# A deeper opening: normalise, transpose and values in three successive turns

## The chip, the cores and the metric

The kernel runs on one core of one Trainium2 chip. The metric is device time in microseconds of one execution. The core's engines work side by side, each in its own order: TensorE (PE, with PEld for its weight loads) multiplies, VectorE (DVE), ScalarE (ACT) and GpSimd (POOL) work on elements, SyncE (SP) issues loads and stores. They wait for each other only through semaphores.

## The reference

A windowed attention over 8 sequences of 576 positions and 8 heads of 64, followed by a feed-forward block with the function h * tanh(softplus(h)) between two weight matrices.

```python
scores = scale * np.matmul(q, k.transpose(0, 1, 3, 2))
mask = (rel >= 0) & (rel < window)          # window = 64
scores = np.where(mask, scores, -1000000000.0)
attn = np.exp(scores - np.max(scores, axis=-1, keepdims=True))
attn = attn / (np.sum(attn, axis=-1, keepdims=True) + 1e-09)
attn_out = np.matmul(attn, v)
...
h = x @ w_in                                # 4608 x 512, 512 x 2048
g = h * np.tanh(np.where(h > 20.0, h, np.log1p(np.exp(np.minimum(h, 20.0)))))
out = g @ w_out                             # 2048 x 512
```

## The kernel before

The 4608 tokens are cut into chunks of 384. For each chunk the attention is computed for four pairs of heads and gives x; then 16 steps, one for each 128 columns of w_in, compute h = x w_in into `h_ps`, apply the function, and add the product with w_out into `acc`. Numbers are kept as two parts, a rounded high one and the remainder (`xh`, `xl`; `gh`, `gl`; two halves of `wi`; `wo_h`, `wo_l`), so each product takes three matmuls.

The weights come as 64-bit numbers and are made into such pairs on the chip, one piece of 128 x 512 after another, by `stream()`. A piece takes: a scaling on ACT (`w_scale`), a shift and a clamp on DVE (`w_ready`, TENSOR_SCALAR), two joins on DVE (`w_joined`, SCALAR_TENSOR_TENSOR), a rounding to the high part (`w_round`, a CAST), and the difference that is the remainder (`w_rest`, TENSOR_TENSOR wi<-st,wi or wo_l<-st,wo_h), which also issues the load of a later piece into the freed buffer. `some(n)` runs the next n operations of this stream; `OPS[u]` is how many in turn u. The pieces are w_in 0, w_in 1, w_out 0, w_in 2, w_out 1 and so on.

The opening, which is all that the change touches, works through the first two chunks: eight units u = 0 to 7 (chunk, head pair), U = 8. A unit needs

- `products_of(u)`: 24 score matmuls, s_ps (12 instructions); they issue the load of a later unit's q and k once their buffers are free
- `masks(u)`: on DVE six operations that add the mask, scale and find the minimum, pr<-s_ps,masks; `exps(u)`: six exponentials on ACT, which also sum
- `summed(u)`: add of 1e-9 on POOL, reciprocal on DVE, and POOL's multiply pr<-pr,sm of 768 columns
- `transposed(u)` on TensorE (t_ps), `copied(u)` to pT, the first half by ACT, the second by DVE
- `values_of(u)`: 24 matmuls into o_ps; `rest_high(u)` (ACT, xh) and `rest_low(u)` (DVE, xl) cut the result in two parts.

A loop over turns writes these out. Everything here goes through wrappers that keep each engine in the order of the code, so a waiting instruction holds up all that stands behind it on its engine. Between the units, `first_parts` places the matmuls of steps 0 to 2 (`PARTS`: step and number of matmuls) and `step` their functions; step 0 and 1 read x of chunk 0, step 2 x of chunk 1. After the opening the steps follow each other, a step of h_ps, a step of acc.

The functions that the diff touches or that call them:

Of the kernel before, what the change touches and what calls it, by code (L numbers as in the profile page):

```python
# [11 lines left out]
F32 = mybir.dt.float32  # L12
# [4 lines left out]
ALU = mybir.AluOpType  # L17
# [3 lines left out]
OFFSET = 2.0 ** -112  # L21
# [9 lines left out]
def tile_window_attn_mish_ffn(  # L31
# [57 lines left out]
    vec, act, pool, load = (InTurn(e) for e in (nc.vector, nc.scalar, nc.gpsimd, nc.sync))  # L89
# [48 lines left out]
    def in_order():  # L138
        return tc.issue_after(order[-1]) if order else nullcontext()
# [4 lines left out]
    def acc_bank(t, name):  # L144
        return ps_acc.tile([P, CH], F32, name=name, tag=f"acc{t}")

    def h_bank(name, width=CH):
        return ps_h.tile([P, width], F32, name=name, tag="h_ps")
# [5 lines left out]
    def at_bank(name, width=CH):  # L154
        at_last[0] = next(at_turn)
        return ps_at.tile([P, width], F32, name=name, tag=f"at{at_last[0]}")

    def at_set(n, name):
        return ps_at.tile([P, DO], F32, name=name, tag=f"at{n}")
# [120 lines left out]
    BY_HEAD = [(h, m) for h in range(2) for m in range(NM)]  # L280
# [107 lines left out]
    def residue():  # L388
        while residues:
            gl, t, gh = residues.pop(0)  # L390
            vec.tensor_tensor(gl, t, gh.bitcast(F32), ALU.subtract)
# [48 lines left out]
    def w_load():  # L440
        if pieces:
            fn, f = pieces.pop(0)
            loaded.append(fn(f))
# [25 lines left out]

    def w_rest(piece):  # L470
        lo, hi, wh, wl = piece
        vec.tensor_tensor(wl, lo.bitcast(F32), wh.bitcast(F32), ALU.subtract)
        w_load()
        yield

# [19 lines left out]
    def scaled_by(engine):  # L495
        return lambda out, in_: engine.tensor_scalar(out, in_, OFFSET, None, ALU.mult)

    rounding = []
    by = {"scale": scaled_by(vec), "round": act.copy, "rest": vec}
# [111 lines left out]
    atts = [Att(c) for c in range(PLAIN)]  # L611
# [4 lines left out]
    U = len(units)  # L616
    outs = {}

    def products_of(u):
        a, p = units[u]  # L620
        if u == 0:
            banks = [b for t in range(NM) for b in ([at_bank("s_ps"), at_bank("s_ps")], [acc_bank(0, "s_ps"), acc_bank(1, "s_ps")],
                                                     [h_bank("s_ps"), h_bank("s_ps")])[t]]
        elif u % 2 == 0:
            banks = [acc_bank(t, "s_ps") for t in range(2)]
        else:
            banks = [at_set(i, "s_ps") for i in range(2)]
        a.products(p, banks)
        if u + 3 < U:
            a.load(p + 3, "qk")  # L630
        if u + 2 >= U:
            a.load(p + 2, "qk")

    def values_of(u):
        a, p = units[u]
        o_ps = at_set(0, "o_ps")[:, :CH] if u == U - 1 else acc_bank(2, "o_ps")
        outs[u] = o_ps
        with in_order():
            value_products(a.v[p], a.pT.pop(p), [o_ps[:, n:n + BLK] for n in range(0, CH, BLK)])
        if u + 3 < U:  # L640
            a.load(p + 3, "v")

    def rest_high(u):
        a, p = units[u]
        xh, xl = a.new_x()
        act.copy(xh[:, p, :], outs[u])

    def rest_low(u):
        a, p = units[u]
        xh, xl = a.new_x()  # L650
        vec.tensor_tensor(xl[:, p, :], outs.pop(u), xh[:, p, :].bitcast(F32), ALU.subtract)
# [6 lines left out]
    def step(n, h_ps=None):  # L658
        pend.append((*steps[n], function(h_ps or first_half(n))))
# [2 lines left out]
    atts[0].load(1, "qk")  # L662
    act.preload_act_table_set("exp_and_others")
    atts[0].load(2, "qk")
    w_load()

    def normal_parts(u):
        a, p = units[u]
# [4 lines left out]

    u = 0

    OPS = (0,2,2,2,3,2,2,2,4,3)
    PARTS = {u: ((), ()) for u in range(U + 2)}
    PARTS.update({6: ((), ((0, 3),)), 7: (((0, 4),), ((0, 5),)), 8: (((1, 4),), ((1, 4),)), 9: (((1, 4),), ((2, 12),))})
    RES = 2
    WARM = 5  # L680
    early = []
    ops = stream()

    def some(n):
        for _ in range(n):
            next(ops)

    def summed(u):
        a, p = units[u]
        for _ in normal_parts(u):  # L690
            pass

    def transposed(u):
        a, p = units[u]
        a.te_transpose(p, [acc_bank(h, "t_ps") if u >= U - 2 else h_bank("t_ps") for h in range(2)])

    def copied(u):
        units[u][0].te_copies(units[u][1], (act.copy, vec.tensor_copy))

    def masks(u, squares_=BY_HEAD):  # L700
        a, p = units[u]
        a.masked(p, squares_, exps=False)

    def exps(u, squares_=BY_HEAD):
        a, p = units[u]
        exp(a.pr[p], squares_)
# [11 lines left out]
    def first_parts(u, i):  # L718
        for n, k in PARTS[u][i]:
            first_part(n, k)  # L720
# [4 lines left out]
    def warm(n):  # L725

        with in_order():
            for _ in range(n):
                pe(idle[:, :P], ident, ident, start=True, stop=True)

    warm(WARM)
    atts[0].load(0, "v")
    products_of(0)
    atts[0].load(1, "v")
    products_of(1)
    w_load()
    atts[0].load(2, "v")
    make_identity(nc, ident, nomemset=True)
    masks(0, BY_PAIR)
    exps(0, BY_PAIR)  # L740
    products_of(2)
    w_load()
    for u in range(1, U - 1):
        if u == 1:
            masks(1)
            summed(0)
            by.update(scale=lambda out, in_: act.mul(out, in_, OFFSET), round=pool.tensor_copy, rest=vec)
        else:
            values_of(u - 2)
        if u > 2:  # L750
            summed(u - 1)
        masks(u + 1)
        cut = 6 if u == 2 else 3
        exps(u, BY_HEAD[:cut])
        if u > 1:
            rest_high(u - 2)
        exps(u, BY_HEAD[cut:])
        if u == 1:
            summed(u)
        if 1 < u < U - 2:  # L760
            products_of(u + 2)
        some(OPS[u] - OPS[u] // 2)
        if u > 1:
            rest_low(u - 2)
        some(OPS[u] // 2)
        first_parts(u, 0)
        transposed(u - 1)
        copied(u - 1)
        if u == 1:
            products_of(3)  # L770
        first_parts(u, 1)

    u = U - 1
    values_of(u - 2)
    summed(u - 1)
    exps(u, BY_HEAD[:3])
    rest_high(u - 2)
    exps(u, BY_HEAD[3:])
    rest_low(u - 2)
    first_parts(u, 0)  # L780
    transposed(u - 1)
    copied(u - 1)
    act.preload_act_table_set("mish")
    summed(u)
    some(OPS[u])
    first_parts(u, 1)

    u = U
    values_of(u - 2)
    rest_high(u - 2)  # L790
    rest_low(u - 2)
    first_parts(u, 0)
    transposed(u - 1)
    copied(u - 1)
    step(0, early[0])
    some(OPS[u])
    first_parts(u, 1)

    u = U + 1
    values_of(u - 2)  # L800
    residue()
    rest_high(u - 2)
    rest_low(u - 2)
    first_parts(u, 0)
    step(1, early[1])
    some(OPS[u])
    first_parts(u, 1)
    residue()
    step(2, early[2])
    by.update(scale=lambda out, in_: act.mul(out, in_, OFFSET), round=act.copy, rest=vec)  # L810
# [527 lines left out]
```

## Time and profile before

| | |
|---|---|
| median of 3 runs | 876.76 us (876.74 to 876.89) |
| span of the profiled execution | 876.1 us |
| its own time | not listed beside its span; the runs are 0.7 us above the span |
| TensorE busy | 863.6 us, 99% |
| DVE, ACT, POOL busy | 446.3, 456.1, 302.4 us |
| mean granted clock of TensorE | 0.994 |

The span runs from the first to the last instruction. A busy time is the time in which an engine had an instruction running; a matmul's end is modelled, so neighbouring matmuls overlap in the rows. The granted clock is TensorE's, as a share of its full 2.4 GHz.

### The profile page before, as it was taken

The numbers are of one execution on the slowest core, as the hardware profiler recorded it, in microseconds if no ns is written. First come the engines' busy times: TensorE is split into PE (matmuls) and PEld (weight loads), VectorE is DVE, ScalarE is ACT, GpSimd is POOL, SyncE is SP. The second block draws the span as 40 slices with busy tenths as digits, with TensorE's granted clock in tenths as the row PEclk, the third lists the DMA queues.
The fourth block names the chain that finished last, engine by engine and source line by source line (L and its number), as shares of the span: only waits on it lengthen the run. The fifth ranks groups of instructions, "written<-read, shape, count | busy, mean of one in ns | idle before, by whom it ended". The sixth has DMA issues, their size and how long they took to land.

```text
span 876.1 us, 18920 instructions
## 1 busy us (share of the span) xinstructions
PE 863.6 (99%) x7162; PEld 769.6 (88%) x7162; DVE 446.3 (51%) x1258; ACT 456.1 (52%) x1198; POOL 302.4 (35%) x350
## 2 busy tenths in 40 slices
PE   7899999999999999999999999999999999999998
PEld 6698989888898989988888888889889889989896
DVE  6897979557256776342553442545423525322221
ACT  6865666346555666364655563754643635322322
POOL 3410000158656573342242323342333233222311
PEclk7999999999999999999999999999999999999999
DMA  9544354475766686565564655754754442533402
GB/s 308 159 167 163 129 173 141 136 248 189 240 195 232 206 270 191 188 189 174 169 196 157 221 162 164 226 173 148 243 172 142 157 153 88 202 120 114 137 2 73
DMA packets 83755, 151.52 MB, mean 173 GB/s; under 512 B 9008, under 2 KB 59248, under 8 KB 79568
## 3 DMA queue, kind: packets, MB, share of 16 engines
q1 hardware_dynamic: 62224, 64.74, 23.5%
q10 hardware_dynamic: 13968, 65.87, 22.6%
q0 software_dynamic: 7472, 19.70, 6.8%
q8 instruction: 57, 0.93, 0.4%
q14 instruction: 34, 0.28, 0.1%
HBM read 114.36 MB, written 24.12 MB: 158 GB/s over the span
## 4 chain that ended last, share of the span: by engine, by line
PE 97%; DVE 2%; DMA 1%; issue 0%; POOL 0%; ACTq 0%; ACT 0%
PE acc L133 46%; PE m_ps L133 27%; PE h_ps L133 15%; PE s_ps L133 3%; PE at L133 3%; PE o_ps L133 1%; DVE pr L83 1%; DMA k_t<-kT 1%; PE t_ps L341 1%; DVE st L83 0%; DVE pT L83 0%; DVE wi L83 0%; POOL pr L83 0%; DVE xl L83 0%; ACTq L83 0%
## 5 line engine op out<-in xcount | busy, mean ns | idle before, releaser
L1053 POOL TENSOR_TENSOR gl<-t,gh 128x384 fp32r<-128x384 f32 x128 | 130.5, 1021 | 320.6 <-ACT gh L1052 121.6
L133 PE MATMUL acc<-wo_h,gh 128*128 128x512 f32 x576 | 227.2, 399 | 0.0
L133 PE MATMUL acc<-wo_l,gh 128*128 128x512 f32 x576 | 226.1, 393 | 0.0
L133 PE MATMUL acc<-wo_h,gl 128*128 128x512 f32 x576 | 222.7, 391 | 0.0
L133 PE MATMUL m_ps<-wi 128*128 128x384 f32 x1152 | 217.4, 336 | 0.0
L133 PEld LDWEIGHTS m_ps<-wi 128*128 128x128 f32 x1152 | 204.3, 188 | 8.2 <-ACT gh L83 0.2
L133 PE MATMUL h_ps<-xh,wi 128*128 128x384 f32 x512 | 141.1, 338 | 0.0
L133 PEld LDWEIGHTS acc<-wo_h,gl 128*128 128x128 f32 x576 | 108.2, 188 | 24.6
L133 PEld LDWEIGHTS acc<-wo_h,gh 128*128 128x128 f32 x576 | 107.9, 188 | 19.5
L133 PEld LDWEIGHTS acc<-wo_l,gh 128*128 128x128 f32 x576 | 108.3, 188 | 15.4
L83 ACT ACTIVATE pr<-pr,mx 128x96 f32<-128x96 f32 (+1 forms) x288 | 105.7, 372 | 15.5 <-DVE mx L83 14.8
L1048 ACT ACTIVATE gh<-t 128x384 fp32r<-128x384 f32 x96 | 50.4, 525 | 117.8 <-DVE t L1065 79.8
L1065 DVE TENSOR_TENSOR u<-u,m_ps 128x384 f32<-128x384 f32 x64 | 35.2, 550 | 141.7 <-PE m_ps L133 140.9
L1065 DVE TENSOR_TENSOR t<-u,m_ps 128x384 f32<-128x384 f32 x96 | 53.1, 553 | 98.7 <-PE m_ps L133 88.8
L133 PEld LDWEIGHTS h_ps<-xh,wi 128*128 128x128 f32 x512 | 93.5, 188 | 2.6
L133 PE MATMUL h_ps<-xl,wi 128*128 128x384 f32 x256 | 86.2, 337 | 0.0
L83 DVE CUSTOM_DVE_ANT_0 pr<-s_ps,masks 128x96 f32<-128x96 f32 (+1 forms) x264 | 51.1, 258 | 53.3 <-PE s_ps L133 53.3
L83 ACT ACTIVATE t<-h_ps 128x384 f32<-128x384 f32 x64 | 31.4, 491 | 61.6 <-PE h_ps L133 56.6
L83 ACT ACTIVATION_READ_ACCUMULATOR pr<-pr,mx 128x1 f32 x288 | 55.0, 191 | 0.0
L1049 ACT ACTIVATE t<-t 128x384 f32<-128x384 f32 x96 | 50.5, 526 | 8.3
L133 PEld LDWEIGHTS h_ps<-xl,wi 128*128 128x128 f32 x256 | 48.1, 188 | 2.2
L996 POOL DMA_DIRECT2D pT<-tr x74 | 36.9, 503 | 37.1 <-PE m_ps L133 17.1
(81 smaller groups left out, 975.5 us busy)
## 6 DMA issues: line engine op xcount, KB each, us to landing
wi<-sums ACTq DMA_DIRECT2D x32, 1024.0 KB, 5.2
wi<-sums ACTq DMA_DIRECT2D x32, 768.0 KB, 4.3
v_t<-vN SPq DMA_DIRECT2D x16, 768.0 KB, 5.9
st<-w_in SPq DMA_DIRECT2D x16, 512.0 KB, 3.5
st<-w_out SPq DMA_DIRECT2D x16, 512.0 KB, 3.6
k_t<-kT SPq DMA_DIRECT2D x16, 416.0 KB, 6.2
q_t<-qT SPq DMA_DIRECT2D x16, 384.0 KB, 5.6
pT<-tr SPq DMA_DIRECT2D x118, 48.0 KB, 4.7
```

What stands on the lines that cost most here:

```text
L83: i = call(*args, **kw)
L133: i = nc.tensor.matmul(*args, **kw)
L341: order.append(nc.tensor.transpose(t_ps[:, m, :], pr[:, h * NM + m, :], ident).ins)
L996: moves.append(queue.dma_start(pT_all[at:at + TQ, r // TQ].rearrange("p u j q -> p (u j q)"), self.tr[r:r + TQ, i].rearrange("p u j q -> p ...
L1048: nc.scalar.activation(gh, t, AF.Mish)
L1049: nc.scalar.activation(t, t, AF.Mish)
L1053: nc.gpsimd.tensor_tensor(gl, t, gh.bitcast(F32), ALU.subtract)
L1065: nc.vector.tensor_tensor(out_, a, b, ALU.add)
```

## The change

In turn u of the new loop the units stand further apart: the scores of unit u + 2, masks of u + 1, exponentials of u, normalisation of u - 1, transposes of u - 2 and values of u - 3. Before, normalisation, transposes and copies of u - 1 were in one turn and the values of u - 2. There is one more turn (u = 10) and one loop for all. The loads of q and k come ahead of the first weight and values loads, the stream of weights begins in turn 3 instead of 1, and its differences in the opening are done by POOL (`by["rest"]`), after which DVE has them again. The turns' leads are:

```diff
     def w_rest(piece):
         lo, hi, wh, wl = piece
-        vec.tensor_tensor(wl, lo.bitcast(F32), wh.bitcast(F32), ALU.subtract)
+        by["rest"].tensor_tensor(wl, lo.bitcast(F32), wh.bitcast(F32), ALU.subtract)
         w_load()
...
-    OPS = (0,2,2,2,3,2,2,2,4,3)
+    OPS = (0,0,0,2,2,2,3,3,4,4,4)
...
+    for u in range(1, U + 3):
+        if u == 1:
+            masks(1)
+            by.update(scale=lambda out, in_: act.mul(out, in_, OFFSET), round=pool.tensor_copy, rest=pool)
+        if 1 < u < U + 2:
+            transposed(u - 2)
+        first_parts(u, 0)
+        if u + 2 < U:
+            products_of(u + 2)
+        if u in (1, 3):
+            w_load()
+        if u == 1:
+            atts[0].load(2, "v")
+        if u + 1 < U:
+            masks(u + 1, BY_HEAD[:3])
+        if u <= U:
+            summed(u - 1)
+        if u + 1 < U:
+            masks(u + 1, BY_HEAD[3:])
+        if u < U:
+            exps(u, BY_HEAD[:3])
+        if 1 < u < U + 2:
+            copied(u - 2)
+        if u > 2:
+            values_of(u - 3)
+        if u < U:
+            exps(u, BY_HEAD[3:])
+        if u > 2:
+            rest_high(u - 3)
+        if u == U - 1:
+            act.preload_act_table_set("mish")
+        some(OPS[u] - OPS[u] // 2)
+        if u > 2:
+            rest_low(u - 3)
+        some(OPS[u] // 2)
...
+        first_parts(u, 1)
```

How this moves instructions shows at three places. The first is POOL from the rounding of the second piece on, before the change (sm<-sm is the add, pr<-pr,sm the multiply, CAST a rounding):

```order
L83 CAST wi<-st 128x512
L83 TENSOR_SCALAR sm<-sm 128x6
L83 TENSOR_TENSOR pr<-pr,sm 128x768
L83 TENSOR_SCALAR sm<-sm 128x6
L83 TENSOR_TENSOR pr<-pr,sm 128x768
L83 TENSOR_SCALAR sm<-sm 128x6
L83 TENSOR_TENSOR pr<-pr,sm 128x768
L83 CAST wo_h<-st 128x512
L83 CAST wi<-st 128x512
```

and on POOL after the change, from the rounding of the first piece on:

```order
L83 CAST wi<-st 128x512
L83 TENSOR_SCALAR sm<-sm 128x6
L83 TENSOR_TENSOR pr<-pr,sm 128x768
L83 TENSOR_TENSOR wi<-st,wi 128x512
L83 TENSOR_SCALAR sm<-sm 128x6
L83 TENSOR_TENSOR pr<-pr,sm 128x768
L83 CAST wi<-st 128x512
L83 TENSOR_TENSOR wi<-st,wi 128x512
L83 TENSOR_SCALAR sm<-sm 128x6
L83 TENSOR_TENSOR pr<-pr,sm 128x768
L83 CAST wo_h<-st 128x512
L83 TENSOR_TENSOR wo_l<-st,wo_h 128x512
```

Between the multiplies there are now roundings and differences; the add and multiply of unit 6 stand behind the first difference, those of unit 7 behind the second rounding and difference. The second place is TensorE at the first three matmuls of step 0, before the change (t_ps are the transposes of unit 5, o_ps the values of units 4 and 5):

```order
L133 MATMUL o_ps<-pT,v_t 64x64 x12
L341 MATMUL t_ps<-ident,pr 128x128 x6
L133 MATMUL h_ps<-xh_308,wi 128x384
L133 MATMUL h_ps<-xl_309,wi 128x384
L133 MATMUL h_ps<-xh_308,wi 128x384
L133 MATMUL o_ps<-pT,v_t 64x64 x12
```

and on TensorE after (o_ps are the values of unit 3, t_ps again the transposes of unit 5):

```order
L133 MATMUL o_ps<-pT,v_t 64x64 x12
L133 MATMUL h_ps<-xh_363,wi 128x384
L133 MATMUL h_ps<-xl_364,wi 128x384
L133 MATMUL h_ps<-xh_363,wi 128x384
L341 MATMUL t_ps<-ident,pr 128x128 x6
```

The three matmuls, of which the third reads the first piece's difference, moved ahead of the transposes. The third place is DVE from the copy of unit 7's transposes to the last remainder xl, before:

```order
L83 COPY pT<-t_ps 128x3x4x32
L83 TENSOR_SCALAR st<-st 128x512
L83 TENSOR_TENSOR wo_l<-st,wo_h 128x512
L83 SCALAR_TENSOR_TENSOR st<-st 128x512 x2
L83 TENSOR_TENSOR gl<-t,gh 128x384
L83 TENSOR_TENSOR xl_564<-o_ps,xh_563 128x384
```

and on DVE after, from the copy of unit 6's transposes on:

```order
L83 COPY pT<-t_ps 128x3x4x32
L83 SCALAR_TENSOR_TENSOR st<-st 128x512 x2
L83 TENSOR_TENSOR xl_591<-o_ps,xh_590 128x384
L83 TENSOR_SCALAR st<-st 128x512 x2
L83 COPY pT<-t_ps 128x3x4x32
L83 SCALAR_TENSOR_TENSOR st<-st 128x512
L83 TENSOR_TENSOR xl_591<-o_ps,xh_590 128x384
L83 SCALAR_TENSOR_TENSOR st<-st 128x512
L83 TENSOR_SCALAR st<-st 128x512
L83 TENSOR_TENSOR gl<-t,gh 128x384 x2
L83 TENSOR_SCALAR st<-st 128x512
L83 TENSOR_TENSOR xl_591<-o_ps,xh_590 128x384
```

The remainders of the last three units now stand between weight operations of two more pieces, and two gl differences stand ahead of the last.

## Rows read from the trace of the kernel before

**Rows 1.** The page: busy us, share of span, instructions.

```profile
PE 863.6 (99%) x7162; PEld 769.6 (88%) x7162; DVE 446.3 (51%) x1258; ACT 456.1 (52%) x1198; POOL 302.4 (35%) x350
```

**Rows 2.** TensorE's waits, whole span: us in total, times, longest.

```profile
PE t_ps L341 <- POOL pr L83: 3.0, 2, 2.2
PE o_ps L133 <- ACT pT L83: 1.6, 3, 1.0
PE o_ps L133 <- DVE pT L83: 1.5, 4, 0.4
PE idle L133 <- DVE ident L83: 1.1, 1, 1.1
PE s_ps L133 <- DMA k_t<-kT: 1.0, 1, 1.0
```

**Rows 3.** Stretches: length, busy us (instructions) by engine, granted clock, DMA share, GB/s.

```profile
12.00:22.30 10.30, 9.63 (x118) 7.75 (x111) 7.58 (x34) 6.00 (x26) 3.14 (x5) 0.50 1.07 349
22.30:33.00 10.70, 7.69 (x138) 5.94 (x137) 10.30 (x50) 9.66 (x41) 5.69 (x6) 1.00 0.74 215
42.30:72.00 29.70, 29.70 (x154) 27.16 (x151) 28.02 (x55) 18.43 (x35) 3.99 (x7) 1.00 0.46 162
```

**Rows 4.** TensorE in order of time: start, us, instruction [idle before, releaser].

```profile
10.30 0.88 PE L341 MATMUL t_ps<-ident,pr 128*128 128x128 f32 x6 [2.21 <-POOL pr L83]
...
14.70 1.56 PE L133 MATMUL s_ps<-k_t,q_t 64*64 64x128 f32 x24
16.19 1.54 PE L341 MATMUL t_ps<-ident,pr 128*128 128x128 f32 x6
...
24.15 0.89 PE L133 MATMUL s_ps<-k_t,q_t 64*64 64x128 f32 x24
24.97 0.88 PE L341 MATMUL t_ps<-ident,pr 128*128 128x128 f32 x6
...
29.37 0.88 PE L341 MATMUL t_ps<-ident,pr 128*128 128x128 f32 x6
...
39.97 0.88 PE L341 MATMUL t_ps<-ident,pr 128*128 128x128 f32 x6
...
44.89 0.34 PE L133 MATMUL h_ps<-xl,wi 128*128 128x384 f32 x1
...
45.24 0.39 PE L133 MATMUL acc<-wo_h,gh 128*128 128x512 f32 x1
...
47.30 0.33 PE L133 MATMUL h_ps<-xh,wi 128*128 128x384 f32 x1
```

**Rows 5.** DVE and POOL side by side, in order of time.

```profile
23.27 0.25 DVE L83 CUSTOM_DVE_ANT_0 pr<-s_ps,masks 128x128 f32<-128x128 f32 x1
23.44 1.47 POOL L83 TENSOR_TENSOR pr<-pr,sm 128x768 f32<-128x768 f32 x1 [1.45 <-DVE sm L83]
24.50 0.96 DVE L83 TENSOR_TENSOR wi<-st,wi 128x512 fp32r<-128x512 f32 x1
...
37.93 0.65 DVE L83 SCALAR_TENSOR_TENSOR st<-st 128x512 uint32<-128x512 uint32 x1
38.17 1.75 POOL L83 TENSOR_TENSOR pr<-pr,sm 128x768 f32<-128x768 f32 x1 [0.45 <-DVE sm L83]
38.50 1.70 DVE L83 TENSOR_SCALAR st<-st 128x512 uint32<-128x512 uint32 x1
...
41.69 0.68 DVE L83 TENSOR_TENSOR wo_l<-st,wo_h 128x512 fp32r<-128x512 f32 x1
```

**Rows 6.** POOL: two groups of 3 to 45 us (count, busy, mean ns), two later instructions.

```profile
L83 POOL CAST wi<-st 128x512 fp32r<-128x512 f32 x3 | 2.6, 872 | 3.0 <-DVE st L83 3.0
L83 POOL TENSOR_SCALAR sm<-sm 128x6 f32<-128x6 f32 x8 | 2.3, 284 | 9.1 <-ACT pr L83 9.0
...
257.90 1.03 POOL L83 TENSOR_TENSOR gl<-t,gh 128x384 fp32r<-128x384 f32 x1
281.19 1.84 POOL L955 TENSOR_TENSOR xn<-xn 128x768 f32<-128x768 f32 x1 [1.92 <-ACT xn L951]
```

**Rows 7.** DVE at the end of the opening.

```profile
42.29 1.41 DVE L83 SCALAR_TENSOR_TENSOR st<-st 128x512 uint32<-128x512 uint32 x2
44.09 0.55 DVE L83 TENSOR_TENSOR xl<-o_ps,xh 128x384 fp32r<-128x384 f32 x1
```

More of the change, by code (lines that the diff above doesn't have):

```diff
@@ L664, in tile_window_attn_mish_ffn @@
     atts[0].load(2, "qk")
-    w_load()
     def normal_parts(u):
@@ L674, in tile_window_attn_mish_ffn @@
     u = 0
-    OPS = (0,2,2,2,3,2,2,2,4,3)
-    PARTS = {u: ((), ()) for u in range(U + 2)}
-    PARTS.update({6: ((), ((0, 3),)), 7: (((0, 4),), ((0, 5),)), 8: (((1, 4),), ((1, 4),)), 9: (((1, 4),), ((2, 12),))})
+    OPS = (0,0,0,2,2,2,3,3,4,4,4)
+    PARTS = {u: ((), ()) for u in range(U + 3)}
+    PARTS.update({6: ((), ((0, 3),)), 7: (((0, 4),), ((0, 5),)), 8: (((1, 4),), ((1, 4),)), 9: (((1, 4),), ()), 10: ((), ((2, 12),))})
+    STEPS = (8, 9)
     RES = 2
@@ L731, in tile_window_attn_mish_ffn @@
     warm(WARM)
+    products_of(0)
+    products_of(1)
     atts[0].load(0, "v")
[L733 to L737, printed above, removed]
     make_identity(nc, ident, nomemset=True)
@@ L742, in tile_window_attn_mish_ffn @@
     w_load()
-    for u in range(1, U - 1):
+    atts[0].load(1, "v")
+    for u in range(1, U + 3):
         if u == 1:
             masks(1)
[L746 to L749, printed above, removed]
-        if u > 2:
[L751 to L761, printed above, removed]
+            by.update(scale=lambda out, in_: act.mul(out, in_, OFFSET), round=pool.tensor_copy, rest=pool)
[18 more added lines that the diff above has]
+            copied(u - 2)
+        if u > 2:
+            values_of(u - 3)
[5 more added lines that the diff above has]
+            act.preload_act_table_set("mish")
@@ L762, in tile_window_attn_mish_ffn @@
         some(OPS[u] - OPS[u] // 2)
-        if u > 1:
-            rest_low(u - 2)
+        if u > 2:
+            rest_low(u - 3)
         some(OPS[u] // 2)
[L766 to L770, printed above, removed]
-        first_parts(u, 1)
[L773 to L807, printed above, removed]
+        if u in STEPS:
+            n = STEPS.index(u)
+            step(n, early[n])
+            if n:
+                residue()
```

## The prediction

> **What bounds the kernel now.** I read the page's busy times first, then who TensorE waited for, then stretches, then single turns. TensorE is busy 99% of the span [rows 1], and all its waits that have a named releaser come to 8.2 us, every one before 40 us: 3.0 for POOL's normalised scores, 3.1 for the copies of the transposes, 1.0 for a load, 1.1 at the start [rows 2]. From 42.3 to 72 us it is busy 29.70 of 29.70 us [rows 3], and it stays so to the end. What a new opening is worth is therefore one difference: where the stream without waits begins. I use the first h_ps matmul of step 3, at 47.30 us [rows 4], as the mark; what moves it moves the end.
>
> Two things stretch the opening today. The granted clock is half from 12.0 to 22.3 us, after TensorE had waited 2.2 us for the first normalised unit [rows 3, 4]; a unit's 24 score matmuls take 1.56 us there and 0.89 after, its transposes 1.54 and 0.88 [rows 4]. And each turn holds a chain: reciprocal, POOL's multiply, transpose, copies, values. At full clock the transposes start at 24.97, 29.37 and 39.97 us [rows 4], so the last four turns take (39.97 - 24.97) / 4 = 3.75 us each, for 2.7 us of TensorE's work (three groups of 0.9). The change aims at this chain.
>
> **What the change removes and adds.** TensorE has the same matmuls, only in another order. DVE loses four weight differences, POOL gains them. The first weight operation moves from turn 1 to turn 3. The loads of q and k come ahead of the first weight and values loads on SP's queue.
>
> *Loads.* TensorE waits 1.0 us for the second unit's keys [rows 2]. Nothing the change moves stands ahead of those, so I take nothing for it; the values of unit 0 and the first weights, now queued behind the q and k of units 3 to 5, have no reader before turn 3 either. DMA is full from 12 to 22.3 us [rows 3]: if the loads of units 5 to 7 were late, the bound is the 1 us that one load costs now, and the cover is the slack of two turns.
>
> *The lock between DVE and POOL.* It decides the rest. POOL's multiply runs 23.44 to 24.91, and the difference that DVE starts at 24.50 takes 0.96 us; at 41.69, with POOL idle, the same operation takes 0.68. A shift on DVE, started at 38.50 under the multiply of 38.17 to 39.92, takes 1.70, and that multiply took 1.75 because the operation of 37.93 was still running [rows 5]. Six mask operations pass under a multiply at 0.205 us each (23.27 to 24.50), unhindered. So weight operations and POOL's work take turns, scores don't. The Trainium skill says the same and more strongly (SBUF — State Buffer, Who interferes with whom): a DVE instruction with two SBUF inputs, or in a two-port mode, and a GpSimd instruction that reads SBUF exclude each other for the whole instruction. By that rule a difference on POOL holds up all DVE's weight work for its whole length, which speaks against this edit; the rows show it for the multiply alone.
>
> *Price of a difference on POOL.* The trace has no such instruction. POOL's two-input operations take 1.03 us for 384 columns and 1.84 for 768 [rows 6], so 0.0021 us a column and 1.30 for 512. Bounds: 1.03 (as short as 384 columns) to 1.84. I take 1.3, on the line between the two. On DVE it cost 0.68 free and 0.96 under a multiply, so the four cost DVE some 3.3 us and will cost POOL 5.2.
>
> *Turns 1 to 3.* The reciprocal of unit 0 now stands behind three more masks (0.6 us), so its multiply ends at about 10.9 instead of 10.3 [rows 4]. But TensorE has the scores of unit 3 meanwhile, its pauses are under 1 us, and I expect the full clock here. Without weights, masks and exponentials run ahead: I place the multiply of unit 3 at 17.9 to 19.4 and its transposes at 19.4, 5.5 us earlier than 24.97.
>
> *Turns 4 to 8.* From here each turn is a loop. While a multiply holds the lock (1.47), DVE does three masks and a copy, then waits; after it come a weight operation 0.6, a remainder 0.5, another weight operation 0.6, three masks 0.6 and the reciprocal 0.3, and only then the next multiply: 1.5 + 2.6 = 4.1 us. On POOL alone a turn with add 0.3, gap 0.3, multiply 1.5, rounding 0.87 [rows 6] and difference 1.3 is 4.3. So the turn gets no shorter than the 3.75 of before, it gets longer. Multiply 4 ends at 23.5, multiply 5 at 27.2. Then the new order bites: the three first h_ps matmuls stand ahead of the transposes of unit 5, and the third needs the first difference, which POOL gives only after multiply 5: 27.2 + 0.5 (DVE's turn at the lock) + 1.3 = 29.0. TensorE stands still 3.3 us with those transposes queued behind, and with them both copies and the next values. The transposes of unit 5 start at 29.1, those of unit 6 at 32.4, of unit 7 at about 36.0, against 39.97: of 5.5 us gained, 4 are left.
>
> *The tail.* The last remainder xl on DVE, which the step-2 matmuls read, ends now at 44.64 (44.09 + 0.55) [rows 7], 4.7 us after unit 7's transposes began. In the new order DVE is behind: multiply 6 ends at 31.3, then rounding 0.87, difference 1.3, add 0.3 on POOL with gaps of 0.2 give 34.2, then reciprocal and copy 6 to 34.8. From there to the last remainder DVE has four joins, 0.61 each (1.41 for two, less 0.1 each of overlap), four shifts and clamps 0.36 each, one copy, two gl differences and three remainders at 0.47: 2.4 + 1.4 + 2.8 = 6.7 us (nearest rows: [rows 7]), 41.5 without a lock. In the same stretch POOL holds the lock for the end of multiply 7 (0.9), two differences (2.6) and one rounding (0.87): 4.4 us, and DVE's copy and remainders, 1.9 us of the 6.7, can pass under them only where they happen to fall. Bounds: 41.5 (all hidden: 3.1 us earlier than now) to 45.9 (none hidden: 1.3 later). The order puts three or more lock operations after each remainder, which is nearer to the second; I take 45.7, 1.1 later than now. Today step 2's matmul that reads it starts at 44.89 [rows 4], 0.25 after it; with a wait in its place it starts at 45.75 or so, 0.9 later. After it come the same nine matmuls of the first sum.
>
> **Sum.** Mark at 47.30 + 0.9 or 1.0 = 48.3. The profiled span is 876.1, the runs' median 876.76, so 0.7 us lie around the span: 876.1 + 0.7 + 1.0 = 877.8 us. That is +0.11%, below the 0.2% (1.75 us) that I count as telling apart from no change.
>
> **Rivals.** *The clock falls at the new stall (slower).* TensorE pauses 3.3 us before the transposes of unit 5; before the fall at 12.0 it had paused 2.2 [rows 2, 3], so a fall at about 29 us is likely. For some turns it is covered, since a turn at half clock is 4.6 us of TensorE's work against the 4.1 to 4.3 of the loop. It decides if it lasts until 41 us: then step 1's rest and step 2, some 15 matmuls of 0.17 us (0.35 for the two from 44.89 to 45.24 [rows 4]), at half clock cost up to 2.5 us more; part lies under the wait for DVE, so I take 2.3. 877.8 + 2.3 = 880.1. The Trainium skill (TensorE: Matmul & The Clock Gate, What's actually happening) has TensorE at half rate after idleness and back after sustained work; by that rule the time would be this rival's. For it: the fall that the trace shows; against it: half clock makes TensorE busier, and it came back at 22.3 in such work.
>
> *The lock is lighter than I take it (faster).* If joins, which no row shows waiting for POOL, can run under a difference, or differences take 1.03, half of the 4.4 us goes, and the last remainder ends at 43.5. The mark then moves by up to the 2 us that other work allows: 876.8 - 2.0 = 874.8. It decides from a hold of under 1.5 us in the tail. For it: the order leaves DVE four operations fewer; against it: the lengthened operations of [rows 5].
>
> *The early clock falls after all.* With the half clock from about 12 us, TensorE needs 4.6 us for each of turns 2 to 4, and the 5.5 us gained shrink to 3; the mark moves to about +2.3 over now, more where it lasts: 879.8.
>
> **Chances.** Forecast (876.9 to 878.5) 0.45; later clock fall 0.22; lighter lock 0.2; early fall 0.13. The later fall ends in part inside 0.2%, and the forecast's upper edge only just, so: faster by over 0.2% 0.2, within 0.45, slower 0.35. The range reaches from a little past the lighter lock, 874.6, to 880.4, which takes in both falls, save their longest forms.
>
> **What the profile would show.** Right: the transposes of unit 3 near 19.4, of unit 7 near 36, a wait of about 3 us of TensorE on POOL's wi before unit 5's transposes, DVE shifts or joins of over 1 us beside POOL's differences of 1.2 to 1.4, a wait of TensorE on DVE's xl in step 2, and nothing changed after 48 us. Wrong: differences near 1 us, or joins that run at 0.6 under them; half clock in the first 20 us; no wait at step 2; a wait on wo_l or wi in steps 3 to 5, which have over 1 us of slack by this count.

## The result: 1.07% slower

885.78 us (884.26 to 886.45, 4 runs) against 876.75 for the kernel before: ratio 1.0107, 95% interval [1.0095, 1.0119]. I had forecast 877.8, and a range up to 880.4. The span of the profiled execution is 884.6 us against 876.1 before.

The five largest waits of TensorE in the changed kernel, over the whole span (total, how many, longest). Before, the waits with a named releaser were 8.2 us in all [rows 2], none of them after 40 us:

```profile
engine line waited for: us in total, times, longest us
PE s_ps L133 <- DMA k_t<-kT: 3.4, 3, 2.5
PE h_ps L133 <- DVE xl L83: 2.5, 1, 2.5
PE h_ps L133 <- POOL wi L83: 2.3, 1, 2.3
PE t_ps L341 <- POOL pr L83: 1.9, 3, 0.9
PE s_ps L133 <- ACT gh L83: 1.9, 1, 1.9
```

TensorE's timeline in the changed kernel, which answers to [rows 4]:

```profile
start us, us, engine line op out<-in xcount [idle before <-releaser]
19.49 0.89 PE L133 MATMUL s_ps<-k_t,q_t 64*64 64x128 f32 x24 [2.52 <-DMA k_t<-kT]
...
21.66 1.54 PE L341 MATMUL t_ps<-ident,pr 128*128 128x128 f32 x6
...
31.00 0.69 PE L133 MATMUL h_ps<-xh,wi 128*128 128x384 f32 x1 [2.34 <-POOL wi L83]
31.48 1.48 PE L341 MATMUL t_ps<-ident,pr 128*128 128x128 f32 x6
...
39.13 0.82 PE L341 MATMUL t_ps<-ident,pr 128*128 128x128 f32 x6
...
47.62 0.54 PE L133 MATMUL h_ps<-xl,wi 128*128 128x384 f32 x1 [2.50 <-DVE xl L83]
47.96 0.52 PE L133 MATMUL h_ps<-xh,wi 128*128 128x384 f32 x1
48.28 0.63 PE L133 MATMUL acc<-wo_h,gh 128*128 128x512 f32 x1
...
51.72 0.34 PE L133 MATMUL h_ps<-xh,wi 128*128 128x384 f32 x1
```

Read it against the forecast: the transposes of unit 3 at 21.66 (forecast 19.4), of unit 7 at 39.13 (36), the matmul that reads the last xl at 47.62 (45.75), the mark at 51.72 (48.3; before 47.30). Behind the wait for xl stand the nine matmuls of the first sum. The first eight start 0.43 us apart and the ninth 0.23 behind them; before, all stood 0.23 apart [rows 4]. The granted clock of that stretch is 0.56 on average, that is half clock for most of it:

```profile
core 0: us, PE busy (x) PEld busy (x) DVE busy (x) ACT busy (x) POOL busy (x), PEclk, DMA share, GB/s
12.00:22.30 10.30, 7.37 (x139) 6.06 (x138) 7.14 (x41) 8.58 (x37) 5.44 (x6) 0.91 1.05 352
22.30:33.00 10.70, 7.28 (x93) 5.93 (x92) 9.38 (x37) 8.92 (x38) 7.35 (x7) 0.82 0.85 252
...
48.00:51.70 3.70, 3.70 (x11) 2.97 (x10) 3.63 (x8) 2.02 (x4) 1.31 (x3) 0.56 0.25 97
```

The mark moved by 4.4 us, the span by 8.5. So 4.1 us are lost behind the mark, where I had expected nothing. The row for it is the wait for `gh` of 1.9 us. ScalarE and TensorE there, in the changed kernel (the scores are those of the third chunk, between two sums):

```profile
117.49 0.67 ACT L83 ACTIVATE st<-st 128x512 f32<-128x512 f32 x1 [2.15 <-DMA st<-w_out]
118.06 0.47 ACT L83 ACTIVATE t<-h_ps 128x384 f32<-128x384 f32 x1
118.43 0.48 ACT L83 ACTIVATE gh<-h_ps 128x384 fp32r<-128x384 f32 x1
...
116.39 0.70 PE L133 MATMUL s_ps<-k_t,q_t 64*32 64x96 f32 x24
118.96 0.74 PE L133 MATMUL s_ps<-k_t,q_t 64*32 64x96 f32 x24 [1.87 <-ACT gh L83]
119.63 0.80 PE L133 MATMUL acc<-wo_h,gh 128*128 128x512 f32 x1
120.22 0.63 PE L133 MATMUL acc<-wo_l,gh 128*128 128x512 f32 x1
120.65 0.63 PE L133 MATMUL acc<-wo_h,gl 128*128 128x512 f32 x1
...
123.31 0.34 PE L133 MATMUL h_ps<-xh,wi 128*128 128x384 f32 x1
```

ScalarE waits 2.15 us for a load of weights with the scaling of that piece; the function's `t` and `gh` stand behind it, and the second half of the scores waits until `gh` is done. After the wait most of the sum runs at half clock again (0.43 apart; granted clock 0.50 from 119.6 to 122.8 us).

### The profile page after: what moved, and what is told of

It is laid out like the page before. It is cut to its first block, busy times and chain, and to the rows that moved or that the text cites. A ratio compares the mean times of both kernels' runs of the same rounds, so it can differ in the third digit from the quotient of the medians.

```text
span 884.6 us, 18922 instructions
## 1 busy us (share of the span) xinstructions
PE 866.3 (98%) x7162; PEld 772.4 (87%) x7162; DVE 449.9 (51%) x1254; ACT 454.6 (51%) x1198; POOL 307.9 (35%) x354
## 4 chain that ended last, share of the span: by engine, by line
PE 91%; DVE 4%; DMA 2%; ACT 2%; POOL 1%; issue 0%; ACTq 0%; SPq 0%; POOLq 0%
PE acc L133 44%; PE m_ps L133 27%; PE h_ps L133 13%; PE at L133 3%; PE s_ps L133 3%; DVE st L83 2%; DMA k_t<-kT 1%; PE o_ps L133 1%; DMA st<-w_out 1%; DVE pr L83 1%; DVE gl L83 1%; ACT pr L83 0%; POOL pr L83 0%; ACT L83 0%; PE t_ps L341 0%; DVE xl L83 0%
## 5 line engine op out<-in xcount | busy, mean ns | idle before, releaser
L133 PEld LDWEIGHTS acc<-wo_h,gh 128*128 128x128 f32 x576 | 108.7, 189 | 19.9 <-issue 0.2
```

Source lines behind the costliest of these rows:

```text
L133: i = nc.tensor.matmul(*args, **kw)
```

## The experiments

The names: a_ is the changed kernel with an edit, b_ the kernel before with one. Three numbers of each trace turned out to tell nearly everything: when the transposes of unit 3 start (t3), how long it is from there to the matmul that reads the last xl (d), and the span less the mark (what comes behind the opening). The ratio is to the kernel before, with its 95% interval; 0.001 is 0.88 us. The ratio rests on all runs of a kernel, the other columns on one trace each, and t3 varies between traces: seven runs with the same order up to unit 3 (changed kernel, a_ops22, a_ops23, a22_parts, a_rest_dve, a_tail, a_tail2) have it from 20.75 to 23.05. The first three of them have the same order up to the last xl, and d from 25.8 to 26.7.

| run | ratio | t3 | d | mark | span - mark |
|---|---|---|---|---|---|
| before | 1 | 24.97 | 19.9 | 47.30 | 828.8 |
| b_rest_pool (a repetition) | 0.9999 [0.9989, 1.0008] | 22.91 | 19.9 | 45.22 | 828.6 |
| b_rest_pool2 | 1.0011 [1.0002, 1.002] | 23.18 | 20.2 | 45.82 | 829.3 |
| b_ops24 | 1.0067 [1.0051, 1.0084] | 23.28 | 19.9 | 45.60 | 835.3 |
| changed kernel | 1.0107 [1.0095, 1.0119] | 21.66 | 26.0 | 51.72 | 832.9 |
| a_ops22 | 1.0062 [1.0041, 1.0084] | 22.41 | 25.8 | 50.74 | 829.2 |
| a_ops23 | 1.0063 [1.0049, 1.0077] | 20.91 | 26.7 | 50.17 | 829.0 |
| a_wload | 1.0158 [1.0143, 1.0173] | 25.44 | 26.6 | 54.52 | 833.4 |
| a22_wload | 1.0084 [1.0069, 1.0099] | 20.54 | 27.5 | 52.11 | 829.0 |
| a22_parts | 1.0073 [1.0058, 1.0088] | 20.75 | 25.8 | 50.56 | 828.8 |
| a_rest_dve | 1.0091 [1.0075, 1.0106] | 21.34 | 24.2 | 49.42 | 832.7 |
| a_tail | 1.0025 [1.0012, 1.0037] | 21.04 | 22.6 | 46.13 | 828.7 |
| a_tail_loads | 1.0039 [1.0025, 1.0052] | 23.35 | 22.9 | 48.73 | 828.9 |
| a_tail2 | 1.0018 [1.0008, 1.0028] | 23.05 | 22.5 | 48.13 | 829.0 |
| a_v2 | 1.0018 [1.0009, 1.0027] | 21.02 | 22.5 | 46.09 | 829.0 |
| a_v12 | 1.0021 [1.0012, 1.003] | 21.73 | 22.5 | 46.77 | 829.1 |
| a_early | 1.0029 [1.0018, 1.0041] | 23.83 | 20.2 | 46.57 | 829.0 |
| a_loads_early | 1.0017 [1.0008, 1.0026] | 23.13 | 20.4 | 46.05 | 828.7 |

### Behind the opening: the phase of the weight stream

**a_ops22.** Two weight operations fewer in the last turn.

```diff
-        some(OPS[u] // 2)
+        some(OPS[u] // 2 if u < U + 2 else 0)
```

> The changed kernel, with two weight operations fewer in its last turn (22 in the opening, as before the change, instead of 24). Theory A (the order of the weight stream against the steps): with 24 the scaling of a piece stands on ScalarE directly ahead of the next function (t, gh) and its wait for a load holds up the scores of the third chunk at about 117 us (TensorE waited 1.87 us there and then ran at half clock for about 3 us). With 22 that wait is gone and about 4.1 us come back: about 881.7 us. The wait at the first sum (DVE's last xl, 2.5 us) stays. Theory B (the weight stream is merely late because the opening is late): the wait near 117 us stays, within 0.5 us of the changed kernel's 885.8, or gets longer, as two operations more have to be done later.

881.0 us (879.84 to 884.2). Span less mark goes from 832.9 to 829.2, and the wait for `gh` is gone. The same scores in a_ops22, on ScalarE and TensorE:

```profile
113.44 0.49 ACT L83 ACTIVATE t<-h_ps 128x384 f32<-128x384 f32 x1 [0.18 <-PE h_ps L133]
113.83 0.48 ACT L83 ACTIVATE gh<-h_ps 128x384 fp32r<-128x384 f32 x1
115.28 0.69 ACT L83 ACTIVATE st<-st 128x512 f32<-128x512 f32 x1 [0.97 <-DMA st<-w_out]
...
115.39 0.93 PE L133 MATMUL s_ps<-k_t,q_t 64*32 64x96 f32 x48
...
118.43 0.33 PE L133 MATMUL h_ps<-xh,wi 128*128 128x384 f32 x1
```

The scaling still waits for its load (0.97 us), but the function now stands ahead of it, so nobody waits for the wait. From the first of these scores to the next h_ps matmul it takes 3.0 us (115.39 to 118.43), in the changed kernel 6.9 (116.39 to 123.31): 3.9 of the 4.1 us. Theory A holds.

Why two operations do that: each later step issues the function of that step and then the next five operations of the stream. A piece is scaled with the second join of the piece ahead of it, and that one is rounded with the scaled piece's shift. With 22 operations done, a step's five are join, scaling and join, rounding and shift, clamp, difference: ScalarE has function, scaling, rounding, function. With 24 they begin two later, at the rounding, and ScalarE has function, rounding, scaling, function.

**b_ops24.** The same step on the kernel before, the other way.

```diff
-    OPS = (0,2,2,2,3,2,2,2,4,3)
+    OPS = (0,2,2,2,3,2,2,2,4,5)
```

> The kernel before, with two weight operations more in its last turn (24 instead of 22), nothing else. Theory A (order of the stream against the steps): the scaling now stands ahead of the function on ScalarE here too, a wait of TensorE for ScalarE's gh of 1 to 2 us appears at the scores of the third chunk near 112 us, with half clock behind it: 878 to 881 us. Theory B (lateness of the opening): no such wait, since this opening is as early as before: 876.0 to 877.5 us.

882.49 us (880.81 to 882.77): 5.9 us slower by the ratio, with an opening as early as in the repetition of the kernel before (mark 45.60 and 45.22). Two waits for `gh` appear, on ScalarE and TensorE:

```profile
54.53 0.69 ACT L83 ACTIVATE st<-st 128x512 f32<-128x512 f32 x1 [1.61 <-DMA st<-w_out]
55.11 0.48 ACT L83 ACTIVATE t<-h_ps 128x384 f32<-128x384 f32 x1
55.48 0.48 ACT L83 ACTIVATE gh<-h_ps 128x384 fp32r<-128x384 f32 x1
...
56.02 0.44 PE L133 MATMUL h_ps<-xh,wi 128*128 128x384 f32 x1 [1.92 <-ACT gh L83]
...
114.86 0.70 PE L133 MATMUL s_ps<-k_t,q_t 64*32 64x96 f32 x24 [1.73 <-ACT gh L83]
```

Theory B falls: the opening isn't late here. The time is above what either theory expected; I had counted one wait where there are two.

**a_ops23.** One operation fewer than in the changed kernel.

```diff
-        some(OPS[u] // 2)
+        some(OPS[u] // 2 if u < U + 2 else 1)
```

> The changed kernel with 23 weight operations in the opening, between 22 (881.0 us) and 24 (885.8). With 23 the scaling of a piece stands first in each step's five operations, behind the function (t, gh) on ScalarE, and the rounding ahead of the next function; with 24 the rounding is first and the scaling stands ahead of the next function. Theory A1 (it is the scaling's wait for its load ahead of the function that costs): 23 is like 22, 880 to 882 us, with no wait of TensorE for gh at the scores of the third chunk. Theory A2 (every operation that the opening does more shifts the stream and costs its part): about half way, 883 to 884.

881.27 us (880.54 to 882.62), span less mark 829.0: like 22, not half way. It is the place of the scaling in the step that costs, not the number of operations done early.

### The loads of the first 20 us

**a_wload and a22_wload.** The first three loads of weights later; then, with 22 operations, only the second and third.

```diff
 a_wload:
-    w_load()
     atts[0].load(1, "v")
...
-        if u in (1, 3):
+        if u in (2, 3, 4):
 a22_wload (with the edit of a_ops22):
-        if u in (1, 3):
+        if u in (2, 4):
```

> The changed kernel, with the first three loads of weights (512 KB each) issued in turns 2, 3 and 4 instead of before turn 1 and in turns 1 and 3. Theory C (the loads bound the first 20 us): unit 6's keys land 1.5 to 2.5 us earlier than at 19.46 us, TensorE's wait of 2.5 us for them falls below 1, the transposes of unit 3 start near 20 instead of 21.66, and up to 2 us of it reach the end: 883.8 to 885. Theory D (from turn 4 on the loop of DVE and POOL sets the pace): the wait for the keys shrinks but the transposes of unit 7 stay within 0.5 us of 39.1 and the time within 0.5 us of 885.8.

890.12 us (888.73 to 890.68), outside both theories. TensorE's wait for the keys of unit 6 fell from 2.52 to 1.34, but the first piece came late; DVE waited 6.67 us for it, with the xl of unit 0 behind it, and TensorE's values behind that:

```profile
18.28 0.89 PE L133 MATMUL s_ps<-k_t,q_t 64*64 64x128 f32 x24 [1.34 <-DMA k_t<-kT]
...
22.82 1.55 PE L133 MATMUL o_ps<-pT,v_t 128*64 128x64 f32 x24 [3.66 <-DVE xl L83]
...
21.87 0.43 DVE L83 TENSOR_SCALAR st<-st 128x512 uint32<-128x512 uint32 x1 [6.67 <-DMA st<-w_in]
22.21 0.55 DVE L83 TENSOR_TENSOR xl<-o_ps,xh 128x384 fp32r<-128x384 f32 x1
```

> The changed kernel with 22 weight operations (881.0 us), and with the second and third loads of weights issued in turns 2 and 4 instead of 1 and 3, so that the loads of unit 6's q and k stand ahead of the second weights load on SP's queue; the first load of weights stays where it was. Theory C (the loads of the first 20 us are the bound, in their order): unit 6's keys come 1 to 1.5 us earlier (one load of 512 KB), TensorE's waits for keys of 4.5 us in all fall to 3 or less, the transposes of unit 3 start near 21 instead of 22.4, and up to 1.5 us reach the end: 879.5 to 880.7. Theory D (DVE and POOL set the pace from turn 4 on): the waits for keys shrink, the end stays within 0.5 us of 881.0. Should the second piece come too late, ScalarE waits for it in turn 4 and the time rises by 1 to 3 us.

882.99 us (881.95 to 884.02), 1.9 us more than a_ops22 by the ratios, whose intervals overlap. (By the order of issue it is unit 7's q and k, not unit 6's, that get ahead of the second piece.) The waits for keys were 2.9 us instead of 4.5 and unit 3's transposes came at 20.54, as theory C said, though that is hardly outside the spread of t3. But the second piece came late, ScalarE waiting 1.44 us for it, and d is 27.5 instead of 25.8: the last sentence of the expectation. The matmul that reads the last xl is as late as in a_ops22 (48.01 and 48.21); the mark is 1.4 us later because the clock fell behind the wait for xl here and not there. In both runs the load that is put back is waited for.

**a_v2 and a_v12.** Values later, on top of a_tail2 (below).

```diff
 a_v2:
-        if u == 1:
+        if u == 2:
             atts[0].load(2, "v")
 a_v12 (and the load of unit 1's values ahead of the loop is gone):
+        if u in (1, 2):
+            atts[0].load(u, "v")
```

> The run a_tail2 (878.1 us) with the load of unit 2's values a turn later, behind the loads of unit 7's q and k; they are read at about 25 us and were loaded by 19. Theory C3 (the loads bound the first 20 us by their bytes: 393 KB at the 350 GB/s of this stretch are 1.1 us): TensorE's wait for the keys of unit 6 falls by 0.5 to 1.1 us from 3.1, and the time by 0.4 to 1.1 us, to 877.0 to 877.7. Theory D3 (DVE and POOL set the pace): the wait shrinks, the time stays within 0.3 us of 878.1.

> The run a_v2 with the load of unit 1's values a turn later as well, behind the loads of unit 6's q and k; they are read at about 21 us. Theory C3: the keys of unit 6 come 1.5 to 2.2 us earlier than in a_tail2, the wait for them falls to 1 to 1.5 us, the transposes of unit 3 start near 21 us or earlier, and the time falls to 875.9 to 877.0, which is the level of the kernel before (875.9). Theory D3: the time stays within 0.4 us of 878.1. Should unit 1's values come too late, TensorE waits for v_t before the second unit's values instead and nothing is gained.

877.51 (875.43 to 878.25) and 877.68 us (876.22 to 879.42), by the ratios nothing gained over a_tail2. The wait for unit 6's keys was 3.13 in a_tail2, but 1.67 to 2.52 in the other six runs with that order, so the 2.00 of a_v2 shows no gain. In a_v12 it was 1.55, and the last case came true, TensorE waiting for v_t:

```profile
18.29 0.89 PE L133 MATMUL s_ps<-k_t,q_t 64*64 64x128 f32 x24 [1.55 <-DMA k_t<-kT]
20.88 0.92 PE L133 MATMUL o_ps<-pT,v_t 128*64 128x64 f32 x24 [1.70 <-DMA v_t<-vN]
```

In no run did t3 come before 20.5, and no run on the loads gained time.

### From unit 3 to the last xl: DVE and POOL

**a_rest_dve.** The differences back on DVE.

```diff
-round=pool.tensor_copy, rest=pool)
+round=pool.tensor_copy, rest=vec)
```

> The changed kernel, with the four weight differences of the opening on DVE instead of POOL. Theory E (the lock: a difference on POOL holds up DVE's weight work for its 1.4 to 1.7 us): shifts and joins that took 1.9 to 2.6 us for two go back to 0.8 and 1.4, the third h_ps matmul starts about 1.4 us earlier than 31.0, and the last xl ends 0.5 to 1.5 us earlier than 47.56: 883.5 to 885.3 us. Rival (DVE is the fullest engine and four more operations of 0.7 us lengthen its queue): the last xl ends 1 to 2.5 us later, 886.5 to 888 us.

883.52 us (882.99 to 885.92); 1.4 us less than the changed kernel by the ratios, whose intervals overlap, and 2.3 by the marks. d falls from 26.0 to 24.2. The time is what theory E gave, at its low end. The rows of the changed kernel that show the lock, on POOL and DVE:

```profile
29.20 1.74 POOL L83 TENSOR_TENSOR wi<-st,wi 128x512 fp32r<-128x512 f32 x1
...
34.12 1.37 POOL L83 TENSOR_TENSOR wi<-st,wi 128x512 fp32r<-128x512 f32 x1
...
30.18 1.31 DVE L83 SCALAR_TENSOR_TENSOR st<-st 128x512 uint32<-128x512 uint32 x1
...
33.48 2.30 DVE L83 TENSOR_SCALAR st<-st 128x512 uint32<-128x512 uint32 x2
...
44.13 2.57 DVE L83 TENSOR_TENSOR gl<-t,gh 128x384 fp32r<-128x384 f32 x2
```

With POOL idle a join takes 0.68 (at 42.13). In a_rest_dve the two gl of the tail take 1.03, but two shifts and two joins are as long as in the changed kernel or longer, under POOL's multiplies of 31.42 to 32.89 and 35.29 to 36.76:

```profile
31.62 2.35 DVE L83 TENSOR_SCALAR st<-st 128x512 uint32<-128x512 uint32 x2
...
35.49 2.55 DVE L83 SCALAR_TENSOR_TENSOR st<-st 128x512 uint32<-128x512 uint32 x2
...
42.38 1.03 DVE L83 TENSOR_TENSOR gl<-t,gh 128x384 fp32r<-128x384 f32 x2
```

So theory E's step that shifts and joins go back to 0.8 and 1.4 came true in part: the gain is there, the lock with the multiplies stays.

**b_rest_pool and b_rest_pool2.** The differences on POOL in the kernel before. In the first the function still named `vec`, so nothing changed and the run is a repetition: 875.69 us (874.79 to 877.28).

```diff
 b_rest_pool:
-round=pool.tensor_copy, rest=vec)
+round=pool.tensor_copy, rest=pool)
 b_rest_pool2, besides:
-        vec.tensor_tensor(wl, lo.bitcast(F32), wh.bitcast(F32), ALU.subtract)
+        by["rest"].tensor_tensor(wl, lo.bitcast(F32), wh.bitcast(F32), ALU.subtract)
```

> The kernel before, with the four weight differences of the opening on POOL and nothing else changed. Theory E (the lock: a difference on POOL takes 1.4 to 1.7 us and DVE's shifts and joins wait for it): 1 to 3 us slower, 877 to 879, with differences of 1.3 us or more beside joins or shifts of over 1 us. Rival (POOL has the room, and DVE has four operations less in this order): within 0.5 us of 876.0, or up to 1 us faster.

> The kernel before, with the four weight differences of the opening really on POOL (in the run b_rest_pool they had stayed on DVE, so that run was a repetition of the kernel before). Theory E (the lock: a difference on POOL takes 1.4 to 1.7 us and DVE's shifts and joins wait for it): 0.5 to 3 us slower than 875.7, as the changed kernel gained 2.3 us when they went back to DVE. Rival (in the old order POOL is idle between its multiplies and DVE has four operations less, so the price hangs on the changed order): within 0.5 us of 875.7.

b_rest_pool2: 876.92 us (876.35 to 877.78), 1.0 us slower; theory E, at the low end. Its rows, on POOL and DVE:

```profile
23.08 1.75 POOL L83 TENSOR_TENSOR wi<-st,wi 128x512 fp32r<-128x512 f32 x1
...
24.06 1.32 DVE L83 SCALAR_TENSOR_TENSOR st<-st 128x512 uint32<-128x512 uint32 x1
```

The join starts under the difference, which lasts until 24.83, and ends 0.55 after it. This is what the Trainium skill says (SBUF — State Buffer, Who interferes with whom): a DVE instruction with two SBUF inputs and a GpSimd instruction that reads SBUF exclude each other for a whole instruction; here the trace shows it for a difference, which before I had seen for the multiply alone.

**a22_parts.** The first three h_ps matmuls behind the transposes of unit 5, with 22 operations.

```diff
-6: ((), ((0, 3),)), 7: (((0, 4),), ((0, 5),))
+6: ((), ()), 7: (((0, 7),), ((0, 5),))
```

> The changed kernel with 22 weight operations (881.0 us, the run a_ops22), and with the first three h_ps matmuls of step 0 behind the transposes of unit 5 instead of ahead of them. Theory F (the stall of 2.3 to 2.9 us that the prediction priced is on the path): the transposes of unit 5 start near 29.5 instead of 32.0, copies, xl and the end come 1 to 2.5 us earlier, 878.5 to 880. Theory G (from there on DVE and POOL set the pace and TensorE would wait elsewhere): the stall goes, but the last xl ends within 0.7 us of 48.16 and the time is 880.3 to 881.7.

881.85 us (881.11 to 883.23), nothing gained over a_ops22. Of the stall 1.1 us is left (waits for POOL's wi, 2.9 before), TensorE waits 4.1 instead of 1.1 us for POOL's multiplies, and d is 25.8 as without the edit: theory G. The last xl did come 1.7 us earlier in this trace, but only because t3 did; and the clock fell behind the wait for it, as it did not in a_ops22. The stall that I had priced at 3.3 us lay beside the path.

**a_tail, a_tail2.** First: differences on DVE, 22 operations, and the last two behind the last xl. Then also the second gl behind it, and the edit of a22_parts.

```diff
 a_tail (with rest=vec):
-        some(OPS[u] - OPS[u] // 2)
+        if u < U + 2:
+            some(OPS[u] - OPS[u] // 2)
         if u > 2:
             rest_low(u - 3)
```

> The changed kernel with three steps taken back at once: the four differences on DVE again, 22 weight operations instead of 24, and the last two of them behind the last xl on DVE instead of ahead of it. Theory: the three faults found so far (POOL's differences about 2.1 us, order of the stream against the steps about 4.1, weight operations ahead of the last xl 1.3 and the half clock behind TensorE's wait for it 1.5) are all that makes the change slow; they add up to 9.0, and the time falls to that of the kernel before or just under it: the last xl ends near 44.0, 875.2 to 876.8 us. Rival: the wait for loads (3.4 to 5.6 us in every run with this opening) costs as well, and 1 to 3 us over the kernel before stay: 877 to 879.

> The run a_tail (878.2 us) with two more steps taken back: the second gl behind the last xl on DVE, and the first three h_ps matmuls behind the transposes of unit 5. Theory (what stands ahead of the last xl on DVE sets the end): the xl ends 0.5 to 1.5 us earlier than 43.55, TensorE's wait for it falls from 1.2 us to under 0.7, and the time falls by 0.5 to 1.5 us to 876.7 to 877.7. Rival (the end is set by TensorE's waits for keys and for POOL's multiplies earlier on, the rest is slack): within 0.4 us of 878.2.

878.19 (875.77 to 879.48) and 878.09 us (876.05 to 878.94). d is 22.6 and 22.5. Of the 9.4 us by which the changed kernel is slower, all but 1.6 to 2.2 are back. That is the rival of a_tail; and a_tail2 gained nothing over a_tail that the intervals can tell, which is its rival.

**a_tail_loads, a_early, a_loads_early.** The loads in the old order; the stream begun in turn 1 again, on a_v2 (with a load of weights behind `products_of(0)`) and on a_tail_loads.

```diff
 a_early, a_loads_early (of the last entry, the two operations behind the xl are taken):
-    OPS = (0,0,0,2,2,2,3,3,4,4,4)
+    OPS = (0,2,2,2,3,2,2,2,3,2,4)
```

> The run a_tail (878.2 us; differences on DVE, 22 operations, the last two behind the last xl), with the loads in the order of the kernel before: first weights and values ahead of the later q and k. Theory C2 (the bytes that have to come before unit 6's keys are the same, so the order of the loads is worth little): within 0.7 us of 878.2, TensorE's waits for keys 3 to 6 us in all as in a_tail. Rival (q and k first is what lets the scores run ahead): 1 to 3 us slower, with longer waits for keys of units 3 to 5.

> The run a_v2 (877.5 us) with the stream of weights begun in turn 1 as in the kernel before (2, 2, 2, 3, 2, 2, 2, 3, 2, 2 operations) and with the first load of weights issued behind the q and k of unit 3. Theory W (the weight operations left behind unit 3 make the order longer): from the transposes of unit 3 to the matmul that reads the last xl it takes 20 to 21 us instead of 22.5; the transposes of unit 3 come at 21 to 22.5, and the time falls to 874.8 to 876.8. Theory X (the turns themselves are longer, since multiply, transpose and values stand in three turns): it stays at 22 to 23 us, or the transposes of unit 3 come as much later as the rest gets shorter, and the time stays within 0.7 us of 877.5.

> The run a_tail_loads (879.3 us; loads in the order of the kernel before) with the stream of weights begun in turn 1. Theory W: transposes of unit 3 near 23, 20 to 21 us from there to the matmul that reads the last xl, 876.0 to 878.0 us. Theory X: within 0.7 us of 879.3.

a_tail_loads: 879.31 us (879.12 to 879.45), 1.2 us slower than a_tail by the ratios. That is the low end of its rival, but the intervals overlap, so that q and k first is worth something is likely and not shown. a_early: 878.20 us (877.36 to 879.76); d falls to 20.2 as theory W says, but t3 comes at 23.83, TensorE waiting 6.7 us in all for POOL's multiplies: theory X's second case. a_loads_early: 877.12 us (876.47 to 878.37), 1.9 us better than a_tail_loads, nearly all of it in d (22.9 to 20.4): theory W. With a_tail2 and a_v2 it is the best of this opening, and still 0.17% slower than the kernel before. No run beats that one, and what the last 1.5 us are remains open.

## Why the prediction was wrong

The sum of the forecast and the trace, term by term: the forecast's span was 876.1 + 1.0 = 877.1; it is 884.6, so 7.5 us are missing. Two steps of the forecast failed: that what moves the mark moves the end, and that the loads cost nothing. A fall of the clock, which I had as a rival, came on top.

**"And it stays so to the end"; "what moves it moves the end": failed, 4.1 us.** This is the largest step, and one that I had priced at nothing. Alone it does not explain the miss: without it, in a_ops22, the time is 881.0, still above the range's 880.4. I took TensorE's full stretch from 42.3 us on as a property of the program, but it held because ScalarE's queue had the function ahead of the scaling. The change does 24 weight operations in the opening instead of 22. Each later step takes five, so two more shift every later step's order for good. I asked only what the operations cost in the opening. b_ops24 shows it without any of the change's other parts.

**The clock behind the wait for xl: 1.5 us.** From that matmul to the mark it took 4.1 us, instead of the 2.55 that I had taken and 2.4 before [rows 4]. The rival "the clock falls at the new stall" had the mechanism, but at another place: it put the fall behind the stall before unit 5 and its price on steps 1 and 2. There the granted clock was 0.50 from 31.0 to 34.0 us and full again before step 2. What cost was a second fall, behind the wait for xl (0.50 from 48.0 to 51.0), in the nine matmuls of the first sum. It comes and goes between runs: after waits for xl of 2.48 to 2.72 us it came in four traces (changed kernel, a22_wload, a22_parts, a_rest_dve: 3.9 to 4.1 us from xl to the mark) and not in three (a_ops22, a_ops23, a_wload: 2.5 us).

**"Loads: I take nothing": 2.3 us.** I had put the transposes of unit 3 at 19.4; they came at 21.66. Two waits for loads stand ahead of them. TensorE waited 2.52 us for the keys of unit 6, with DMA at 1.05 of its share; behind that wait the granted clock was 0.50 from 20.5 to 23.7 us, and the values ahead of the transposes took 1.42 instead of 0.92. And DVE waited for the first weights, of which I had written that they have no reader before turn 3. In turn 3 they had one, and unit 3's reciprocal stands behind it, so POOL's multiply of unit 3 ended at 20.71, where I had it end by 19.4:

```profile
17.19 0.43 DVE L83 TENSOR_SCALAR st<-st 128x512 uint32<-128x512 uint32 x1 [1.83 <-DMA st<-w_in]
19.24 1.47 POOL L83 TENSOR_TENSOR pr<-pr,sm 128x768 f32<-128x768 f32 x1 [2.41 <-DVE sm L83]
```

So earlier keys alone would have brought the transposes to 20.7 at best. My bound of 1 us was the wait of a slower opening. DMA moved 352 GB/s from 12 to 22.3 us, as before (349 [rows 3]): one that asks for scores sooner meets the same bytes sooner.

**DVE's and POOL's turns, and the tail: right in the sum, for 0.4 us, and in part by luck.** From unit 3's transposes to the xl matmul I had 26.35 us; it took 25.96. But to unit 7's transposes it took 17.5 instead of 16.6, and from there to the xl matmul 8.5 instead of 9.75. A difference on POOL took 1.37 to 1.74, not 1.3. The stall before unit 5, 2.34 us instead of 3.3, was not on the path (a22_parts). What makes d long is, by the runs, weight work on DVE: the differences on POOL with their lock 1.8 us (a_rest_dve), the two last operations ahead of the last xl 1.6 (a_tail), and five operations that a stream begun two turns later leaves behind unit 3, 2.3 to 2.5 (a_early, a_loads_early). The three add to the distance from 26.0 to 20.2, which is nearly the 19.9 of the kernel before.

Together: 4.1 + 1.5 + 2.3 - 0.4 = 7.5, all that is missing between these two traces.

The trace of before was also a late execution, and the 0.7 us that I added around its span was wrong for that reason: each later run has 1.8 us around its span, so the trace's 876.1 would stand for a time of 877.9, 1.1 above the median. Its repetition (b_rest_pool) has the mark at 45.22, and what differs in its rows is the clock. From 12.0 to 22.3 us it was half throughout in the trace that I predicted from [rows 3]; in the repetition it was half from 11.2 to 14.5 only:

```profile
12.00:22.30 10.30, 8.48 (x159) 0.88 1.08 353
```

(length, TensorE busy, granted clock, DMA share, GB/s.) So much of the half clock that "stretches the opening today" was a matter of that one execution. Against the repetition the deeper opening brings unit 3 forward by 1.25 us, not 3.3, while d grows by 6.

Not settled is why a_early and a_loads_early, with the old d, don't keep the t3 of 21: in a_early TensorE waits 6.7 us in all for POOL's multiplies; in a_loads_early 3.5 for keys, 3.4 for the multiplies and 3.1 for DVE's first weight shifts (before the scores at 11.48). I haven't separated weight work from loads there.

## What to carry to other kernels

When a change does more or less of a stream ahead of a loop, work out where each of its operations then stands in the loop's body on every queue, above all one that waits for a load: it belongs behind the work that others wait for. "Busy to the end" is a result of that order, not a bound. And take a stage apart into the time to a fixed point and the distance from there: here the second was the same to 0.1 us in four runs (a_tail, a_tail2, a_v2, a_v12) whose spans differed by 2. And look at a second trace of the kernel before, before a saving is read from the first: here the two differed by 2 us in just the stage that the change aimed at.

## What was not expected of the hardware

A wait of TensorE of some 2 us cost nearly twice its length: 1.87 us at 117 us, and then nine matmuls in 3.7 us (119.63 to 123.31, granted clock 0.50 for most of them) that took 2.2 in a_ops22 without the wait. The Trainium skill has half rate after idleness (TensorE: Matmul & The Clock Gate, What's actually happening); the trace agrees, but not each time: after 2.48 us in a_ops22 the granted clock stayed at 1.00, after 2.48 us in a22_wload it fell.

And the same kernel's opening moved by 2 us between traces (marks at 45.22 and 47.30 for the kernel before), with half clock for 3.3 us in one and for 10.3 in the other. The d of these two traces (19.9) and their span less the mark (828.6 and 828.8) hardly differ.
